# Hand order kept on the matrix engine alone, with a third matmul bank and earlier loads, in a fused windowed-attention and channel-mix kernel

**Chip, cores, metric.** One core of one Trainium2 chip. Times are microseconds (us) on the device. The kernel before took 222.08 us (median of 3 runs, 222.0 to 222.2).

Names: PE is the matrix engine, DVE VectorE, ACT ScalarE, POOL GpSimd, SP SyncE, and DMA a transfer. A *bank* is one of the eight banks of PSUM, the memory that takes PE's results. *Hand order* means that an engine runs its instructions in the order of the source; an engine that is not in hand order gets its order from the Tile scheduler when the program is built.

## The reference, cut

```python
# q, k, v: (4, 8, 768, 64) float32; n_sink 4, window 128
rel  = pos[:, None] - pos[None, :]
keep = (pos < 4) | ((rel >= 0) & (rel < 128))          # sink columns, and the window
a    = softmax(where(keep, q @ k.T / 8, -1e9))
x    = (a @ v), heads side by side                     # (4, 768, 512)
xk   = mu_k * x + (1 - mu_k) * x_prev                  # x_prev: the row before
xr   = mu_r * x + (1 - mu_r) * x_prev
out  = sigmoid(xr @ w_r) * (relu(xk @ w_k) ** 2 @ w_v) # w_k 512x1024, w_v 1024x512, w_r 512x512
```

## The kernel before: the parts that matter

Twelve units (4 batches times 3 blocks of 256 rows) of four attention steps each (c = 0 to 3, two heads a step). The channel mix of a unit is cut into ten chunks, which `fill` puts between the attention steps of the next units, so that PE always has work. The first four chunks, f0 to f3, are the products with w_k (tile mm); ACT makes rl of each and DVE kk. Two chunks give th, and four give the two halves of the output, o_sb. Cuts are marked `# ...`.

```python
tr_ps = ctx.enter_context(tc.tile_pool(name="tr_ps", bufs=2, space=PSUM))
o_ps = ctx.enter_context(tc.tile_pool(name="o_ps", bufs=2, space=PSUM))
mm_ps = ctx.enter_context(tc.tile_pool(name="mm_ps", bufs=2, space=PSUM))   # and sc_ps: 2 banks
# ...
load(0)
# ... constants on POOL, w_k's load on POOL's queue, mu_k and mu_r on ACT's
vs4 = const.tile([32, B, D + 1], FP32, name="vs4")            # v of the sink rows
for h in range(H):
    nc.sync.dma_start(out=vs4[4 * h:4 * h + 4, :, 0:D],
                      in_=v[:, h, 0:NS, :].rearrange("b s d -> s b d"))
# ... in prepare(u, part), for part == 2 of a batch's first unit:
            nc.gpsimd.tensor_tensor(out=vsink[b % 2][0:32, :, :], op=ALU.mult, in0=hmask,
                in1=vs4[:, b:b + 1, :].to_broadcast([32, H, D + 1]))
# ... def mix(u, half): four transposes of x, ACT's copy into xt, then
        td = x_pool.tile([128, 2, 256], BF16, name="td")
        nc.vector.tensor_tensor(out=td, in0=cur, in1=prv, op=ALU.subtract)
        for dst, mu in zip(mixed[u], (mu_k_sb, mu_r_sb)):     # xk twice, then xr twice
            for i in range(2):
                nc.vector.scalar_tensor_tensor(...)
# ...
    with tc.manual_schedule():                                # every engine in source order
        for part in range(4):
            prepare(0, part)
        load(1)
        # ... loads of w_r and w_v
        for n in range(N + LAG):
            u, c = divmod(n, NP)
            # ... sink_scores, scores(n)
            if 2 <= n < N + 2 and c % 2 == 1:
                mix((n - 2) // NP, ((n - 2) % NP) // 2)
            fill(n)
            if n < N:
                masked(n)                                     # DVE: e times the mask
            if 1 <= n < N + 1:
                values(n - 1)                                 # PE: o; DVE: rec, x
            fill(n)
            if n < N and u + 1 < U:
                prepare(u + 1, c)
                if c == 3 and u + 2 < U:
                    load(u + 2)
            if c % 2:
                fill(n)
            # ... n == 4: wv_h = 0.5 * wv_sb, eight DVE instructions
```

The softmax here doesn't subtract the row's maximum and nothing guards it: scores larger than these inputs give would overflow.

## Time and profile before

| what | value |
|---|---|
| time; span of the profiled run | 222.1; 220.4 us |
| PE busy | 180.1 us (82%) |
| first channel-mix matmul of unit 0 (its first f0) | 39.32 us |
| from there to the f0 of unit 11 | 168.23 us |
| from there to the end | 12.85 us |

The three last rows are first f0, stretch between the f0s, and tail. They are start times of the first matmul of w_k in a unit, read from PE's order of time. The lines of the profile stand in the prediction.

### The profile page before, as it was taken

How to read it: one execution, taken by the hardware profiler on the slowest of the kernel's cores; microseconds unless marked ns; L12 is line 12 of the kernel's file. 1: busy time of each engine (PE TensorE's matmuls, PEld its weight loads, DVE VectorE, ACT ScalarE, POOL GpSimd, SP SyncE). 2: the span in 40 equal slices, each digit the busy share in tenths (PEclk: the TensorE clock that was granted, in tenths of full speed). 3: DMA queues.
4: the chain of work that ended last, by engine and by line, in shares of the span. 5: the costliest groups of instructions: out<-in, count | busy, mean ns of one | idle time of the engine just before them, and what ended most of it. 6: DMA issues, size and time to landing. Idle time of an engine off the chain costs nothing.

```text
span 220.4 us, 4299 instructions
## 1 busy us (share of the span) xinstructions
PE 180.1 (82%) x1664; PEld 120.9 (55%) x1664; DVE 140.9 (64%) x344; ACT 124.9 (57%) x201; POOL 34.4 (16%) x69
## 2 busy tenths in 40 slices
PE   1705706999898898996997998988998989979892
PEld 1403405675765755854755757657557557555550
DVE  0011634976786678659669757857866696697632
ACT  2402703694675675774764956855757748555250
POOL 8736011223002001032020020050020200000000
PEclk9999985799999999999999999999999999999998
DMA  7979999950591991951782945915908911020202
GB/s 128 213 142 220 179 221 209 221 97 3 146 202 37 218 166 49 216 120 49 179 157 97 206 83 150 210 26 154 222 24 213 156 49 48 3 95 0 75 23 95
DMA packets 81668, 28.10 MB, mean 127 GB/s; under 512 B 76528, under 2 KB 78064, under 8 KB 81648
## 3 DMA queue, kind: packets, MB, share of 16 engines
q1 hardware_dynamic: 78496, 25.20, 52.6%
q0 software_dynamic: 2096, 2.62, 6.9%
q8 instruction: 13, 0.21, 0.4%
q10 hardware_dynamic: 1056, 0.00, 0.3%
q14 instruction: 7, 0.06, 0.1%
HBM read 24.15 MB, written 6.29 MB: 138 GB/s over the span
## 4 chain that ended last, share of the span: by engine, by line
PE 50%; DVE 16%; ACT 12%; DMA 11%; SPq 5%; issue 4%; ACTq 0%; DVEq 0%
PE mm L274 19%; PE mm L286 9%; DMA ks<-in_k_dram 6%; PE tps L151 6%; PE mm L294 6%; DVE xr L261 5%; SPq L69 4%; DMA vs<-in_v_dram 4%; ACT e L194 4%; DVE xk L261 4%; DVE o_sb L299 3%; PE sc L190 3%; ACT xt L253 3%; ACT rl L278 3%; DVE td L255 3%
## 5 line engine op out<-in xcount | busy, mean ns | idle before, releaser
L274 PE MATMUL mm<-xk,wk_sb 128*128 128x256 bf16 x384 | 50.1, 275 | 12.9 <-DVE o_sb L299 8.5
L194 ACT ACTIVATE e<-sc 128x1024 bf16<-128x1024 f32 (+1 forms) x48 | 46.0, 958 | 9.0 <-PE sc L190 9.0
L294 PE MATMUL mm<-wv_h,kk 128*128 128x512 bf16 x192 | 48.3, 379 | 0.0
L274 PEld LDWEIGHTS <-wk_sb 128*128 128x128 bf16 x384 | 36.4, 98 | 19.1 <-issue 14.6
L278 ACT ACTIVATE rl<-mm 128x512 bf16<-128x512 f32 x48 | 29.1, 607 | 29.2 <-PE mm L274 29.2
L156 POOL CAST v<-vs 128x512 bf16<-128x512 f32 x24 | 15.9, 664 | 139.5 <-DMA vs<-in_v_dram 83.7
L154 ACT CAST kt<-tps 128x512 bf16<-128x512 f32 x24 | 14.1, 586 | 41.5 <-PE tps L151 41.5
L255 DVE TENSOR_TENSOR td<-xt 128x512 bf16<-128x512 bf16 x24 | 10.6, 440 | 40.1 <-ACT xt L253 40.1
L151 PE MATMUL tps<-ident,ks 128*128 128x128 f32 x96 | 17.4, 312 | 20.1 <-DMA ks<-in_k_dram 20.1
L151 PEld LDWEIGHTS tps<-ident,ks 128*128 128x128 f32 x96 | 13.4, 161 | 24.3 <-issue 15.3
L286 PE MATMUL mm<-wr_sb,xr 128*128 128x512 bf16 x96 | 24.4, 380 | 0.0
L294 PEld LDWEIGHTS <-kk 128*128 128x128 bf16 x192 | 16.9, 98 | 13.1
L261 DVE SCALAR_TENSOR_TENSOR xk<-td,mu_k_sb,xt 128x256 bf16<-128x256 bf16 x48 | 23.2, 524 | 0.9
L279 DVE TENSOR_TENSOR kk<-rl 128x512 bf16<-128x512 bf16 x48 | 20.2, 421 | 5.4 <-ACT rl L278 3.9
L227 PE MATMUL o<-v,e 128*128 128x65 bf16 x352 | 21.0, 196 | 1.9 <-DVE e L203 1.3
L203 DVE TENSOR_TENSOR e<-e,mask 128x768 bf16<-128x768 bf16 x16 | 8.8, 551 | 21.5 <-ACT e L194 21.5
L200 DVE TENSOR_TENSOR e<-e,mask 128x1024 bf16<-128x1024 bf16 x32 | 22.3, 697 | 0.0
L261 DVE SCALAR_TENSOR_TENSOR xr<-td,mu_r_sb,xt 128x256 bf16<-128x256 bf16 x48 | 21.7, 492 | 0.0
L227 PEld LDWEIGHTS <-e 128*128 128x128 bf16 x352 | 17.7, 99 | 7.0 <-DVE e L200 1.9
L232 DVE TENSOR_TENSOR x<-o,rec 128x256 bf16<-128x256 f32 x48 | 20.4, 424 | 1.6
L190 PE MATMUL sc<-qt,kt 64*128 64x128 bf16 (+1 forms) x256 | 19.1, 251 | 0.7 <-ACT qt L154 0.7
L299 DVE SCALAR_TENSOR_TENSOR o_sb<-th,mm 128x512 f32<-128x512 f32 x24 | 16.2, 678 | 3.5 <-PE mm L294 3.5
(42 smaller groups left out, 166.6 us busy)
## 6 DMA issues: line engine op xcount, KB each, us to landing
ks<-in_k_dram SPq DMA_DIRECT2D x24, 256.0 KB
qs<-in_q_dram SPq DMA_DIRECT2D x24, 256.0 KB
vs<-in_v_dram SPq DMA_DIRECT2D x24, 256.0 KB
out_dram<-o_sb SPq DMA_DIRECT2D x24, 256.0 KB
wk_sb<-in_moe_w_k_dram POOLq DMA_DIRECT2D x1, 1024.0 KB, 9.7
wv_sb<-in_moe_w_v_dram POOLq DMA_DIRECT2D x1, 1024.0 KB, 13.9
wr_sb<-in_moe_w_r_dram POOLq DMA_DIRECT2D x1, 512.0 KB, 7.9
vs<-in_v_dram SPq DMA_DIRECT2D x8, 4.0 KB
```

Of the source, the lines that this page charges most:

```text
L151: nc.tensor.transpose(out=ps[:, c, :], in_=src[:, g, 2 * c:2 * c + 2, :].rearrange("p a d -> p (a d)"), identity=ident32)
L190: nc.tensor.matmul(out=sc[:, a, o0:o1], lhsT=lhs[rows], rhs=qt[rows, c, q0:q0 + o1 - o0], start=True, stop=True)
L194: nc.scalar.activation(out=e[:, :, lo:], in_=sc[:, :, lo:], func=AF.Exp, scale=scale)
L200: nc.vector.tensor_tensor(out=e, in0=e, in1=mask.rearrange("p a g k q -> p a (g k q)"), op=ALU.mult)
L227: nc.tensor.matmul(out=o[:, g, a, :], lhsT=e[:, a, e0:e0 + 128], rhs=rhs, start=(T == 0 and i == 0), stop=(i == len(blocks) - 1), skip_gro ...
L232: nc.vector.tensor_tensor(out=xs[u][:, :, 128 * c:128 * c + 128].rearrange("p g (a d) -> p g a d", a=2), in0=o[:, :, :, 0:D], in1=rec.to_b ...
L261: nc.vector.scalar_tensor_tensor(out=dst[:, c0 + i, :], in0=td[:, i, :], scalar=mu[:, c0 + i:c0 + i + 1], in1=prv[:, i, :], op0=ALU.mult, ...
L274: nc.tensor.matmul(out=ps[:, i, :], lhsT=wk_sb[:, c, 128 * f:128 * f + 128], rhs=xk[:, c, :], start=(c == 0), stop=(c == NC - 1), skip_gro ...
L278: nc.scalar.activation(out=rl, in_=ps, func=AF.Relu)
L286: nc.tensor.matmul(out=ps, lhsT=xr[:, c, 128 * g:128 * g + 128], rhs=wr_sb[:, c, :], start=(c == 0), stop=(c == NC - 1))
L294: nc.tensor.matmul(out=ps, lhsT=kk[:, f, 128 * g:128 * g + 128], rhs=wv_h[:, f, :], start=(f == 0), stop=(f == NF - 1))
L299: nc.vector.scalar_tensor_tensor(out=o_sb, in0=th[g], scalar=1.0, in1=ps, op0=ALU.add, op1=ALU.mult)
```

## The change

Its intent: leave only PE in hand order, let the Tile scheduler order the rest; bring load(1) forward; get the sink rows of v from tiles that are loaded anyway, by a matmul with a 0/1 matrix, instead of eight small loads and a POOL product; and give the channel mix a third bank, taken from o. In the source xk and xr are split, and xr is placed one step later.

```diff
-    o_ps = ... bufs=2        mm_ps = ... bufs=2
+    o_ps = ... bufs=1        mm_ps = ... bufs=3
     load(0)
+    load(1)
 ...
-    vs4 = ...; for h in range(H): nc.sync.dma_start(out=vs4[...], ...)
 ...
-            nc.gpsimd.tensor_tensor(out=vsink[b % 2][0:32, :, :], op=ALU.mult, in0=hmask, in1=vs4...)
+    def sink_values(b):
+        ps = tr_ps.tile([128, H, D], FP32, name="tps")
+        nc.tensor.matmul(out=ps, lhsT=spread, rhs=v_bufs[b * NT % 3][:, 0, :, 0:D], ...)
+        nc.vector.tensor_tensor(out=vsink[b % 2][0:32, :, 0:D], in0=ps[0:32], op=ALU.mult, in1=hmask...)
 ...
-    with tc.manual_schedule():
+    ORDERED = {mybir.EngineType.PE}
+    with tc.manual_schedule(engines=ORDERED):
 ...
-                mix((n - 2) // NP, ((n - 2) % NP) // 2)
+                transposed((n - 2) // NP, ((n - 2) % NP) // 2)
             fill; masked(n); values(n - 1)
+            if c % 2 == 1 and 2 <= n < N + 2:
+                mix((n - 2) // NP, ((n - 2) % NP) // 2, 0)          # td, xk
             fill
-                prepare(u + 1, c)
+                ... for u == 0 all four parts at c == 3, else prepare(u + 1, c)
+            if c % 2 == 0 and 3 <= n < N + 3:
+                mix((n - 3) // NP, ((n - 3) % NP) // 2, 1)          # xr, a step later
+            if c == 2 and inner and u % NT == 0:
+                sink_values(u // NT)
+            if n == 0: the loads of w_r and w_v
+            if n == 5: wv_h                                        # was n == 4
```

More of the change, by code (lines that the diff above doesn't have):

```diff
@@ L54 @@
     tr_ps = ctx.enter_context(tc.tile_pool(name="tr_ps", bufs=2, space=PSUM))
-    o_ps = ctx.enter_context(tc.tile_pool(name="o_ps", bufs=2, space=PSUM))
-    mm_ps = ctx.enter_context(tc.tile_pool(name="mm_ps", bufs=2, space=PSUM))
+    o_ps = ctx.enter_context(tc.tile_pool(name="o_ps", bufs=1, space=PSUM))
+    mm_ps = ctx.enter_context(tc.tile_pool(name="mm_ps", bufs=3, space=PSUM))
     raw = {}
@@ L107 @@
     nc.scalar.dma_start(out=mu_r_sb, in_=moe_mu_r.rearrange("(c p) -> p c", p=128))
-    vs4 = const.tile([32, B, D + 1], FP32, name="vs4")
-    for h in range(H):
-        nc.sync.dma_start(out=vs4[4 * h:4 * h + 4, :, 0:D],
-                          in_=v[:, h, 0:NS, :].rearrange("b s d -> s b d"))
     nc.gpsimd.memset(mask, 1.0)
@@ L129 @@
         nc.gpsimd.memset(t, 0.0)
-    hmask = const.tile([32, H, D + 1], FP32, name="hmask")
+    hmask = const.tile([32, H, D + 1], BF16, name="hmask")
     nc.gpsimd.memset(hmask, 1.0)
@@ L135 @@
                             pattern=[[4, H], [0, D + 1]], channel_multiplier=-1)
-    nc.gpsimd.memset(vs4[:, :, D:D + 1], 1.0)
+    for t in vsink:
+        nc.gpsimd.tensor_copy(out=t[0:32, :, D:D + 1], in_=hmask[:, :, D:D + 1])
+    spread = const.tile([128, 128], BF16, name="spread")
+    nc.gpsimd.memset(spread, 0.0)
+    nc.gpsimd.tensor_copy(out=spread[0:NS, 0:4 * H].rearrange("p (h s) -> p h s", s=NS),
+                          in_=ident[0:NS, 0:NS].unsqueeze(1).to_broadcast([NS, H, NS]))
     kts, qts = {}, {}
@@ L156, in prepare @@
             nc.gpsimd.tensor_copy(out=v_bufs[u % 3][:, g, :, 0:D], in_=vs[:, g, :, :])
-        if part == 2 and T == 0:
+        if part == 3 and T == 0:
             kz = ksink[b % 2].rearrange("p (c w) -> p c w", w=136)
@@ L162, in prepare @@
                                       in_=kts[u][rows, 0, :, 0:NS])
-            nc.gpsimd.tensor_tensor(
-                out=vsink[b % 2][0:32, :, :], op=ALU.mult, in0=hmask,
-                in1=vs4[:, b:b + 1, :].to_broadcast([32, H, D + 1]))
+    def sink_values(b):
+        ps = tr_ps.tile([128, H, D], FP32, name="tps")
+        nc.tensor.matmul(out=ps, lhsT=spread, rhs=v_bufs[b * NT % 3][:, 0, :, 0:D],
+                         start=True, stop=True)
+        nc.vector.tensor_tensor(out=vsink[b % 2][0:32, :, 0:D], in0=ps[0:32], op=ALU.mult,
+                                in1=hmask[:, :, 0:D])
     es, xs, live = {}, {}, {}
@@ L237, with transposed @@
     mixed = {}
-    def mix(u, half):
+    def transposed(u, half):
         b, T = divmod(u, NT)
@@ L250, in mix @@
         t0 = 2 + 256 * T
-        cur = xt[:, c0:c0 + 2, t0:t0 + 256]
+        nc.scalar.copy(out=xt[:, c0:c0 + 2, t0:t0 + 256], in_=ps)
+    def mix(u, half, which):
+        b, T = divmod(u, NT)
+        xt = xts[b % 2]
+        c0 = 2 * half
+        t0 = 2 + 256 * T
         prv = xt[:, c0:c0 + 2, t0 - 1:t0 + 255]
-        nc.scalar.copy(out=cur, in_=ps)
-        td = x_pool.tile([128, 2, 256], BF16, name="td")
-        nc.vector.tensor_tensor(out=td, in0=cur, in1=prv, op=ALU.subtract)
-        if half == 0:
+        if half == 0 and which == 0:
             mixed[u] = (x_pool.tile([128, NC, 256], BF16, name="xk"),
-                        x_pool.tile([128, NC, 256], BF16, name="xr"))
-        for dst, mu in zip(mixed[u], (mu_k_sb, mu_r_sb)):
-            for i in range(2):
-                nc.vector.scalar_tensor_tensor(
-                    out=dst[:, c0 + i, :], in0=td[:, i, :], scalar=mu[:, c0 + i:c0 + i + 1],
-                    in1=prv[:, i, :], op0=ALU.mult, op1=ALU.add)
+                        x_pool.tile([128, NC, 256], BF16, name="xr"),
+                        x_pool.tile([128, NC, 256], BF16, name="td"))
+        td = mixed[u][2][:, c0:c0 + 2, :]
+        if which == 0:
+            nc.vector.tensor_tensor(out=td, in0=xt[:, c0:c0 + 2, t0:t0 + 256], in1=prv,
+                                    op=ALU.subtract)
+        dst, mu = mixed[u][which], (mu_k_sb, mu_r_sb)[which]
+        for i in range(2):
+            nc.vector.scalar_tensor_tensor(
+                out=dst[:, c0 + i, :], in0=td[:, i, :], scalar=mu[:, c0 + i:c0 + i + 1],
+                in1=prv[:, i, :], op0=ALU.mult, op1=ALU.add)
     def ffn(u):
         b, T = divmod(u, NT)
-        xk, xr = mixed[u]
+        xk, xr, _ = mixed[u]
         kk = kk_pool.tile([128, NF, 256], BF16, name="kk")
@@ L310, with fill @@
     chunks = stream()
-    LAG = 6
     N = U * NP
-    def fill(n, count=1):
-        if n >= LAG:
-            for _ in range(count):
-                next(chunks, None)
-    with tc.manual_schedule():
+    def fill(count=1):
+        for _ in range(count):
+            next(chunks, None)
+    ORDERED = {mybir.EngineType.PE}
+    with tc.manual_schedule(engines=ORDERED):
         for part in range(4):
             prepare(0, part)
-        load(1)
-        nc.gpsimd.dma_start(out=wr_sb, in_=moe_w_r.rearrange("(c p) f -> p c f", p=128))
-        nc.gpsimd.dma_start(out=wv_sb, in_=moe_w_v.rearrange("(c p) f -> p c f", p=128))
-        for n in range(N + LAG):
+        for n in range(N + 6):
             u, c = divmod(n, NP)
-            if n < N:
+            inner = n < N
+            if inner:
                 if c == 0 and u % NT > 0:
@@ L330 @@
                 scores(n)
-            if 2 <= n < N + 2 and c % 2 == 1:
-                mix((n - 2) // NP, ((n - 2) % NP) // 2)
-            fill(n)
-            if n < N:
+            if c % 2 == 1 and 2 <= n < N + 2:
+                transposed((n - 2) // NP, ((n - 2) % NP) // 2)
+            if n >= 6:
+                fill()
+            if inner:
                 masked(n)
@@ L337 @@
                 values(n - 1)
-            fill(n)
-            if n < N and u + 1 < U:
-                prepare(u + 1, c)
+            if c % 2 == 1 and 2 <= n < N + 2:
+                mix((n - 2) // NP, ((n - 2) % NP) // 2, 0)
+            if n >= 6:
+                fill()
+            if inner and u + 1 < U:
+                if u == 0 and c == 3:
+                    for part in range(4):
+                        prepare(1, part)
+                elif u > 0:
+                    prepare(u + 1, c)
                 if c == 3 and u + 2 < U:
                     load(u + 2)
-            if c % 2:
-                fill(n)
-            if n == 4:
+            if c % 2 == 0 and 3 <= n < N + 3:
+                mix((n - 3) // NP, ((n - 3) % NP) // 2, 1)
+            if c == 2 and inner and u % NT == 0:
+                sink_values(u // NT)
+            if c % 2 and n >= 6:
+                fill()
+            if n == 0:
+                nc.gpsimd.dma_start(out=wr_sb, in_=moe_w_r.rearrange("(c p) f -> p c f", p=128))
+                nc.gpsimd.dma_start(out=wv_sb, in_=moe_w_v.rearrange("(c p) f -> p c f", p=128))
+            if n == 5:
                 for f in range(NF):
```

## The prediction

> **What bounds the kernel now.** I read the page first, for the shares and the granted clock; then the waits of the matrix engine in the steady stretch; then the order of time around one unit of work; then the start in slices of 1 us.
>
> The kernel runs 12 units (4 batches, 3 blocks of 256 rows), each with 4 attention steps (c = 0 to 3). The channel mix of a unit runs as 10 chunks between the attention steps of the next units: four chunks f0 to f3 (x times w_k, then rl and kk), two of th, and two of o in two halves each.
>
> ```profile
> PE 180.1 (82%) x1664; PEld 120.9 (55%) x1664; DVE 140.9 (64%) x344; ACT 124.9 (57%) x201; POOL 34.4 (16%) x69
> ...
> PE   1705706999898898996997998988998989979892
> ...
> PEclk9999985799999999999999999999999999999998
> DMA  7979999950591991951782945915908911020202
> ```
>
> PE is busy 82% of 220.4 us, and hardly less than 90% anywhere after slice 8 (44 us). So there are two losses: the start, up to about 40 us, and 10% of the rest. By the table of stretches PE is busy 147.7 of the 160 us between 40 and 200: 12.3 us idle. The waits say on what:
>
> ```profile
> PE mm L274 <- DVE o_sb L299: 7.6, 10, 1.4
> PE mm L274 <- ACT rl L278: 4.4, 10, 0.6
> PE o L227 <- DVE e L200: 0.2, 1, 0.2
> ```
>
> That is all of it: two waits per unit, each in front of a chunk f. The order of time in one unit (columns: start, us, engine, line, operation, tiles, idle before):
>
> ```profile
> 83.32 0.51 DVE L255 TENSOR_TENSOR td<-xt 128x512 bf16<-128x512 bf16 x1 [2.17 <-ACT xt L253]
> ...
> 84.67 0.88 DVE L261 SCALAR_TENSOR_TENSOR xr<-td,mu_r_sb,xt 128x256 bf16<-128x256 bf16 x2
> 85.46 0.68 DVE L299 SCALAR_TENSOR_TENSOR o_sb<-th,mm 128x512 f32<-128x512 f32 x1
> ...
> 86.19 1.03 PE L274 MATMUL mm<-xk,wk_sb 128*128 128x256 bf16 x8 [0.56 <-DVE o_sb L299]
> ...
> 87.97 1.03 PE L274 MATMUL mm<-xk,wk_sb 128*128 128x256 bf16 x8 [0.39 <-ACT rl L278]
> ```
>
> DVE does td, xk, xr, o_sb in that order, and f0 starts only when o_sb has emptied a bank. f1 then waits for rl of f0: the allocation of the built program gives f0 and f1 the same bank (in units 1 to 10). PE would have been ready for f0 at 86.19 - 0.56 = 85.63.
>
> The start is bound by loads:
>
> ```profile
> 14.00:15.00 1.00, 0.00 (x0) 0.00 (x0) 0.00 (x0) 0.00 (x0) 0.64 (x2) 1.00 0.38 65
> 15.00:16.00 1.00, 0.00 (x0) 0.00 (x0) 0.00 (x0) 0.00 (x0) 1.00 (x2) 1.00 0.02 4
> 16.00:17.00 1.00, 0.00 (x0) 0.00 (x0) 0.00 (x0) 0.00 (x0) 0.95 (x3) 1.00 0.25 58
> ...
> 33.15 2.12 DVE L348 TENSOR_SCALAR wv_h<-wv_sb 128x512 bf16<-128x512 bf16 x8 [3.38 <-DMA wv_sb<-in_moe_w_v_dram]
> ...
> 35.12 1.09 PE L151 MATMUL tps<-ident,ks 128*128 128x128 f32 x4 [6.63 <-DMA ks<-in_k_dram]
> ```
>
> The last columns of the slices are granted clock, DMA share and GB/s: 65, 4 and 58 GB/s, against some 190 to 275 around them, so about 2.4 us of DMA time are empty. There SP is busy issuing eight small loads of the sink rows (6.90 to 15.4 us), and the second unit's load stands behind them. PE waits 6.63 us for the third unit's ks at 35.12, then runs at half clock until 40.5.
>
> **What the Trainium skill says.** (1) "PSUM — Partial Sum Buffer", Specifications (TRN2): 8 banks per partition. The change spends the same eight: sc 2, tps 2, o 1 instead of 2, mm 3 instead of 2. (2) "SBUF — State Buffer", Who interferes with whom: a DVE instruction with two SBUF inputs contends with a GpSimd instruction that reads SBUF; it is a lock, held for the whole instruction. The trace agrees: beside the 1.43 us vsink product of POOL at 99.07 the pair of xk takes 1.70 us instead of 0.88, and f0 waits 1.35 us instead of 0.56. (3) "DMA: Bandwidth & Descriptors", Queues, rings and completion order: each DMA engine takes turns between the queues. It fits: with POOL's weight loads in flight (20 to 30 us) the sum stays at 189 GB/s, so weights and q, k, v hold each other up. (4) "TensorE: Matmul & The Clock Gate", Part 1: the clock is halved when idle and released by activity. The trace shows 0.50 from 31 to 40.5 us; the change does not remove this.
>
> **The change, part by part.**
>
> *Three mm banks.* In the program as built the banks rotate strictly: f0 takes the bank of th1, f1 that of the first o, f3 that of f0. The waits for o_sb and for rl of f0 before f1 go. What is then left before f0 is xk: its third and fourth matmuls wait for the two xk instructions of the later half.
>
> *The order of DVE.* The Tile scheduler now gives at c = 1: e, o_sb, rec, td, x, xk, xk, o_sb, xr, xr. xk is no longer ahead of e and o_sb, so I count it through with the trace's own spacing: exp ends at 82.81; e 0.61, o_sb 0.61, rec 0.21, td 0.46, x 0.35, xk twice 0.44 end at about 85.5 and 86.0. PE is ready at 85.63; its third and fourth matmuls come 0.21 and 0.32 later, 85.84 and 85.95. So f0 loses about 0.1 us instead of 0.56. Next, the transposes at c = 3 need x of the step before. DVE runs on without a gap: o_sb 0.61, xr 0.80, e 0.61, kk 0.38, rec 0.21, x 0.37 after 86.0 end at 89.0. PE, freed of both waits, would be there at 89.70 - 0.56 - 0.39 = 88.75. So some 0.2 to 0.3 us of the 0.95 come back as a wait for x. Per unit about 0.65 us are won, about 70%.
>
> Waits after 39 us are 8.5 + 4.4 + 0.6 = 13.5 us; 70% is **9.5 us**. The two units slowed by POOL's product (f0 at 102.62 and 149.36, 1.35 us each) are among them; with the product off POOL they become ordinary units.
>
> *Sink rows by matmul.* Four matmuls of 512 columns. Such a matmul costs 0.21 us (0.86 us for four of L286 in the chain), with its weights some 0.25; three lie in the steady stretch: **0.7 us** against us. Four DVE products of about 0.6 us each, beside PE. POOL loses 5.1 us, which is off the path but for the lock.
>
> *One o bank.* o of a step now waits for x of the step before. By the same counting x ends over 1 us before PE comes for the bank: no cost.
>
> *Early loads.* Without the eight small loads the 2.4 us hole fills, and the ks of unit 2 should land about 3 us earlier, near 32. But the scheduler puts four of the eight wv_h instructions ahead of rec and x of step 3 and e of step 4. They wait for wv_sb, which POOL issues only 1.1 us earlier (its vsink product is gone), so it lands near 32.0. Then: wv_h to 33.1, x to 34.0, e to 34.7, the transposes 34.6, xk complete about 38.2, against 39.66 before. Of 3 us, **about 1.6 us** remain.
>
> The tail after the last f0 (207.55 to 220.4) is the same work in the same order.
>
> Sum: 9.5 - 0.7 + 1.6 = 10.4 us off 222.1 gives 211.7; I say **211.5 us**.
>
> **Rivals.** (a) *The scheduler's order gives the gain back.* xk, now behind four other instructions, becomes the new wait before f0 as long as o_sb was. For it: DVE is 64% busy, and more once the units shorten; casts on POOL stretch xk by 0.2 us (1.11 for two at 68.40). Against: the count above leaves only 0.1 us. If f0 still waits 0.5 us and only the rl wait goes, the gain is 4.4 - 0.7 + 1.6: 216.8. (b) *The start gives all of it.* If wv_sb lands before it is needed, the ks arrival rules and 3 to 4 us are won, and with all 13.5 us of waits gone: 222.1 - 13.5 + 0.7 - 3.5 = 205.8. For it: PE is in hand order. Against: wv_h stands early in DVE's order. (c) *The loads are hidden anyway.* The start saves nothing since bytes bound it: 213.3. (d) *The single o bank stalls PE*, at 0.3 us per step, 48 steps: 14 us back, no gain. The slack above speaks against it.
>
> **Range and chances.** The middle of (a) and (b) is about where the sum lies. The range 207.0 to 216.5 leaves out the ends of both. Faster by over 2% means under 217.6, which even (a) reaches: 0.89. Same 0.09, for (d) in part; slower 0.02.
>
> **What would show it right or wrong.** Right: the waits of PE between 40 and 200 name o_sb and rl no more, or under 1 us each; 3 to 4 us remain, on xk and on x before the transposes; one unit takes 14.5 to 14.8 us from f0 to f0, against 15.2 to 16.4; no xk pair of 1.70 us beside POOL; no empty slices at 14 to 17 us; the wait of wv_h ends near 32 and the first f0 near 38. Wrong: waits of o on x (the single bank), a ks or v load late in the steady stretch since the queue's order changed, f0 waiting 0.5 us for xk in each unit, or a start that saves more than 3 us or nothing.

## The result

The changed kernel took 205.31 us (median of 4, 204.83 to 206.94) against 222.14 us of the kernel before on the same chip (4 runs, 222.0 to 222.81). Its outputs are correct. The ratio is 0.925, 95% interval 0.919 to 0.931. Ratios here and below are the mean time of one kernel's fast runs over the mean of the other's in the same rounds, so not quite the ratio of the medians quoted. A run counts as slow when it is over 1.5% above the fastest of its kernel; one kernel that also had slow runs is marked.

So it was faster, as predicted, but 205.3 lies below the range of 207.0 to 216.5: 6.2 us of gain more than I had said. The profiled span fell from 220.4 to 203.1 us:

| | before | after | difference |
|---|---|---|---|
| first f0 | 39.32 | 36.45 | -2.87 |
| to f0 of unit 11 | 168.23 | 153.80 | -14.43 |
| to the end | 12.85 | 12.85 | 0 |

The page of the changed kernel, the same four lines as of before:

```profile
PE 178.5 (88%) x1668; PEld 120.8 (59%) x1668; DVE 135.1 (66%) x348; ACT 125.3 (62%) x201; POOL 32.0 (16%) x68
...
PE   1717706899999999999999999999999999999992
...
PEclk9975755899999999999999999999999999999999
DMA  7999999998895995987879627402011020020202
```

PE worked 1.6 us less than before in a span 17.3 us shorter, so its share rose from 82 to 88%; its row reads 9 from slice 8 (counted from 0, as in the prediction) to the last but one. The DMA row has no 0 or 1 in the first slices. The granted clock still drops in slices 2 to 7; the prediction expected that to stay.

The waits of PE from 30 to 185 us (the columns are the time in total, how often, the longest):

```profile
PE tps L154 <- DMA ks<-in_k_dram: 7.3, 1, 7.3
PE tps L254 <- ACT qt L157: 0.7, 3, 0.2
PE mm L290 <- DVE xk L277: 0.4, 1, 0.4
PE tps L254 <- DVE x L239: 0.3, 1, 0.3
```

No wait for o_sb or rl is left. In the steady stretch 1.4 us remain in all, where the prediction expected 3 to 4. Half of that, the wait for qt, stands behind the three sink matmuls and is absent where these are taken out (a_vs4_between below).

One unit of the changed kernel in order of time, the stretch that answers to 83 to 88 us of the kernel before:

```profile
77.62 0.69 DVE L207 TENSOR_TENSOR e<-e,mask 128x1024 bf16<-128x1024 bf16 x1 [1.70 <-ACT e L201]
...
78.23 0.68 DVE L315 SCALAR_TENSOR_TENSOR o_sb<-th,mm 128x512 f32<-128x512 f32 x1
...
78.82 0.18 DVE L238 RECIPROCAL rec<-o 128x4 f32<-128x4 f32 x1
78.92 0.40 DVE L273 TENSOR_TENSOR td<-xt 128x512 bf16<-128x512 bf16 x1
...
79.23 0.42 DVE L239 TENSOR_TENSOR x<-o,rec 128x256 bf16<-128x256 f32 x1
...
79.56 0.87 DVE L277 SCALAR_TENSOR_TENSOR xk<-td,mu_k_sb,xt 128x256 bf16<-128x256 bf16 x2
...
80.01 0.39 PE L197 MATMUL sc<-qt,kt 64*128 64x256 bf16 x6
...
80.33 1.05 PE L290 MATMUL mm<-xk,wk_sb 128*128 128x256 bf16 x8
...
81.57 1.04 PE L290 MATMUL mm<-xk,wk_sb 128*128 128x256 bf16 x8
...
82.89 0.42 DVE L239 TENSOR_TENSOR x<-o,rec 128x256 bf16<-128x256 f32 x1
...
83.30 0.40 PE L254 MATMUL tps<-ident,x 128*128 128x128 bf16 x4
```

Read DVE's starts. e, o_sb, rec, td, x, xk: this is the order that the prediction took from the built program. But rec starts at 78.82 for 0.18 us, and td already at 78.92, before rec's record ends; x follows td by 0.31. In the kernel before, x stood next to rec and xk next to td, and started 0.21 and 0.55 us after them (86.66 to 86.87, 83.32 to 83.87). Here the independent td starts 0.10 us after rec, and x 0.31 after td, so less of DVE's time passes between the starts. f0 starts at 80.33, 0.32 us after the scores, without a wait. And x for the transposes at c = 3 is done at 82.89 + 0.42 = 83.31, while the transposes start at 83.30: they just meet.

The start, in slices of 1 us as before (last columns: granted clock, DMA share, GB/s), and two lines of the order of time:

```profile
14.00:15.00 1.00, 0.18 (x2) 0.16 (x2) 0.00 (x0) 0.00 (x0) 0.85 (x2) 0.50 1.39 219
15.00:16.00 1.00, 0.09 (x2) 0.00 (x0) 0.00 (x0) 0.00 (x0) 1.00 (x3) 0.50 1.38 217
16.00:17.00 1.00, 0.81 (x8) 0.35 (x7) 0.50 (x2) 0.10 (x1) 0.94 (x5) 0.50 1.39 217
```

```profile
30.27 0.90 DVE L376 TENSOR_SCALAR wv_h<-wv_sb 128x512 bf16<-128x512 bf16 x4 [7.98 <-DMA wv_sb<-in_moe_w_v_dram]
...
32.25 1.09 PE L154 MATMUL tps<-ident,ks 128*128 128x128 f32 x4 [7.29 <-DMA ks<-in_k_dram]
```

The hole at 14 to 17 us is filled: 217 to 219 GB/s instead of 65, 4 and 58. The wait for the third unit's ks ends at 32.25 instead of 35.12, 2.87 us earlier, exactly what the first f0 gained. wv_sb arrived for wv_h at 30.27, not 32.0.

### The profile page after: what moved, and what is told of

Same layout as the page of the kernel before. It is cut to its first block, busy times and chain, and to the rows that moved or that the text cites. A ratio compares the mean times of both kernels' runs of the same rounds, so it can differ in the third digit from the quotient of the medians.

```text
span 203.1 us, 4308 instructions
## 1 busy us (share of the span) xinstructions
PE 178.5 (88%) x1668; PEld 120.8 (59%) x1668; DVE 135.1 (66%) x348; ACT 125.3 (62%) x201; POOL 32.0 (16%) x68
## 4 chain that ended last, share of the span: by engine, by line
PE 67%; DVE 11%; SPq 9%; DMA 7%; ACT 4%; issue 2%; DVEq 0%
PE mm L290 17%; PE mm L310 15%; PE mm L302 11%; SPq L69 9%; PE tps L154 7%; DMA ks<-in_k_dram 7%; PE sc L197 5%; PE o L234 4%; PE tps L254 3%; DVE o_sb L315 3%; DVE xk L277 2%; PE o L223 2%; PE tps L181 2%; ACT e L201 2%; DVE xr L277 2%
## 5 line engine op out<-in xcount | busy, mean ns | idle before, releaser
L201 ACT ACTIVATE e<-sc 128x1024 bf16<-128x1024 f32 (+1 forms) x48 | 45.9, 957 | 14.5 <-PE sc L197 12.7
L290 PEld LDWEIGHTS <-wk_sb 128*128 128x128 bf16 x384 | 34.7, 98 | 6.2 <-issue 1.8
L159 POOL CAST v<-vs 128x512 bf16<-128x512 f32 x24 | 18.1, 767 | 112.6 <-PE o L234 53.7
L234 PEld LDWEIGHTS <-e 128*128 128x128 bf16 x352 | 18.2, 100 | 8.7 <-issue 3.9
L154 PEld LDWEIGHTS tps<-ident,ks 128*128 128x128 f32 x96 | 13.5, 161 | 16.1 <-issue 7.4
L277 DVE SCALAR_TENSOR_TENSOR xk<-td,mu_k_sb,xt 128x256 bf16<-128x256 bf16 x48 | 21.2, 477 | 0.0
L197 PEld LDWEIGHTS <-kt 64*128 64x128 bf16 x256 | 8.9, 95 | 15.2 <-issue 14.6
## 6 DMA issues: line engine op xcount, KB each, us to landing
wv_sb<-in_moe_w_v_dram POOLq DMA_DIRECT2D x1, 1024.0 KB, 12.9
```

The costliest lines, as they stand in the source:

```text
L154: nc.tensor.transpose(out=ps[:, c, :], in_=src[:, g, 2 * c:2 * c + 2, :].rearrange("p a d -> p (a d)"), identity=ident32)
L197: nc.tensor.matmul(out=sc[:, a, o0:o1], lhsT=lhs[rows], rhs=qt[rows, c, q0:q0 + o1 - o0], start=True, stop=True)
L201: nc.scalar.activation(out=e[:, :, lo:], in_=sc[:, :, lo:], func=AF.Exp, scale=scale)
L234: nc.tensor.matmul(out=o[:, g, a, :], lhsT=e[:, a, e0:e0 + 128], rhs=rhs, start=(T == 0 and i == 0), stop=(i == len(blocks) - 1), skip_gro ...
L277: nc.vector.scalar_tensor_tensor(out=dst[:, c0 + i, :], in0=td[:, i, :], scalar=mu[:, c0 + i:c0 + i + 1], in1=prv[:, i, :], op0=ALU.mult, ...
L290: nc.tensor.matmul(out=ps[:, i, :], lhsT=wk_sb[:, c, 128 * f:128 * f + 128], rhs=xk[:, c, :], start=(c == 0), stop=(c == NC - 1), skip_gro ...
```

## The experiments

The first question is what ended the waits for o_sb and rl: the third bank, or the order of DVE? The kernel before with the bank split alone:

```diff
# the kernel before, but
-    o_ps bufs=2, mm_ps bufs=2
+    o_ps bufs=1, mm_ps bufs=3
```

> The kernel before with the bank split of the changed kernel alone (o 1 bank, mm 3), DVE and ACT still in hand order. Theory A, the order theory: the third bank takes away the two waits before f0 and f1, but in the hand order (td, xk, xr, o_sb, e, rec, x, o_sb, kk, e, rec, x without a gap) x of step c = 1 still ends only 0.1 to 0.3 us sooner, and the transposes at c = 3 wait for it; 0.3 us per unit, so 217 to 220 us, with a new wait of the transposes on x of 5 us or more in all. Theory B, the bank theory of the prediction: the waits go and hardly anything comes in their place, 12 to 14 us off, so 208 to 211 us.

Measured: 222.11 us (221.38 to 222.85), ratio 1.001 [0.997, 1.005]. Nothing at all. The waits of PE from 40 to 185 us:

```profile
PE o L216 <- DVE x L232: 10.1, 11, 1.5
PE o L227 <- DVE x L232: 1.8, 3, 0.6
```

The two old waits are gone, and o now waits for x instead, 11.9 us in all: the single o bank is not free, because in the hand order x still comes late. This is my rival (d), which I had dismissed; it is true, but only with the old order of DVE. A third mm bank beside two of o was not run, since the eight banks are spent. The trace of the kernel before leaves little to win by it: DVE works from td at 83.32 to the end of x at 89.53 with no gap over 0.07 us, and the transposes that need this x start at 89.70. Next the reverse, the changed kernel with two mm banks and two of o:

```diff
# the changed kernel, but
-    o_ps bufs=1, mm_ps bufs=3
+    o_ps bufs=2, mm_ps bufs=2
```

> The changed kernel with the banks of before (o 2, mm 2). Theory A (order): o_sb of both halves ends before f0 and f1 come to their banks, so at most 1 us is lost: 205 to 207 us. Theory B (banks): the wait of f0 for o_sb and one more per unit come back, 10 us or more: 214 to 218 us.

Measured: 205.43 us (205.19 to 206.44), ratio 0.9255 [0.923, 0.929], the same as the changed kernel. PE waits from 40 to 185 us for nothing of the channel mix:

```profile
PE tps L254 <- ACT qt L157: 0.7, 3, 0.2
PE tps L254 <- DVE x L239: 0.3, 1, 0.3
```

So this split of the banks is worth nothing with either order. The scheduler alone, on the unchanged source:

```diff
# the kernel before, but
-    with tc.manual_schedule():
+    with tc.manual_schedule(engines={mybir.EngineType.PE}):
```

> The kernel before with hand order on PE alone and nothing else changed (mm 2 banks, sink loads and the product on POOL as before). The built program now rotates the two mm banks strictly (f0 and f1 no longer share one), and DVE does e, td, o_sb, xk, xk, xr, xr, rec, o_sb, x. Theory A (order): o_sb empties the bank before f0 comes, rl of f0 is no longer waited for; nearly all of the 14 us of the steady stretch is won, less some for the product on POOL: 208 to 212 us. Theory B (banks): with two banks the waits of f0 on o_sb and of f1 stay, 219 to 223 us.

Measured: 208.28 us (207.6 to 208.52), ratio 0.937 [0.935, 0.940]. This one line makes some 14 of the 17 us. The first f0 comes at 37.81, the next stretch takes 154.63 us. Which engine's order is it? Only DVE left to the scheduler:

```diff
# the kernel before, but
-    with tc.manual_schedule():
+    with tc.manual_schedule(engines={PE, Activation, Pool, SP})      # of mybir.EngineType
```

> The kernel before in hand order on every engine but DVE, whose order alone the scheduler sets; two mm banks, the old sink rows and loads. Theory A (the gain of the steady stretch is DVE's order, with the bank rotation that follows from it): the waits of PE for o_sb and rl fall from 13 us to under 3, 208 to 212 us. Theory C (it takes ACT, POOL or SP in scheduled order too): 215 us or more.

Measured: 211.69 us (211.07 to 213.33), ratio 0.953 [0.947, 0.959]; first f0 at 38.82, the stretch 157.40 us, so DVE's order alone takes 10.8 us out of it. From 40 to 185 us PE waits for the mm banks still, but little:

```profile
PE mm L274 <- DVE o_sb L299: 3.4, 8, 0.8
```

And the counterpart, all but PE and DVE left to the scheduler:

```diff
# the kernel before, but
+    with tc.manual_schedule(engines={PE, DVE})                       # of mybir.EngineType
```

> The kernel before with hand order on PE and VectorE, and ScalarE, GpSimd and SyncE by the scheduler. The built program still gives f0 and f1 one bank. Order theory: the steady stretch stays as before (12 to 14 us of waits for o_sb and rl after 39 us), only the start may move by 1 us: 220 to 222.5. Rival (the scheduler's order on ScalarE or GpSimd has its own part in the gain): under 218, waits under 9 us.

Measured: 221.26 us (220.31 to 221.85), ratio 0.994 [0.991, 0.998]. The waits from 40 to 185 us are smaller for o_sb than before (6.9 us there, in the same window), but the stretch between the f0s is 167.99 us, hardly shorter:

```profile
PE mm L274 <- DVE o_sb L299: 4.5, 9, 0.7
PE mm L274 <- ACT rl L278: 4.0, 9, 0.6
```

Two waits that are not shown, for x and for e, add 1.1 and 0.9 us. So the gain needs the other order of DVE, and the others' order is worth about 1 us without it and some 3.4 us on top of it (211.69 to 208.28, each against the kernel before).

One rival was left. With DVE scheduled, the built program also deals the two mm banks strictly in turn; with DVE in hand order, f0 and f1 share one (this can be read from the allocation of each built program; the traces fit: in b_dve f1 starts up to 0.44 us before rl of f0 ends, while before it waits for rl in each of units 1 to 10). So DVE's order might work only by way of the banks. The kernel before with strictly alternating banks and everything in hand order:

```diff
# the kernel before, but
-    mm_ps: one pool of 2
+    mm_pools: two pools of 1, taken in turn, tile by tile
```

> The kernel before, in hand order on all engines, with its two mm banks taken strictly in turn (two pools of one buffer). f0 then takes the bank of the first o half, f1 that of the second o half, so f1 no longer waits for rl of f0. If the shared bank was the cause (bank theory), both waits go: 209 to 217 us, rl not named any more, o_sb under 2 us in all. If VectorE's hand order is the cause (order theory): o_sb of the second half ends at 87.89 in the trace of before whatever PE does, since VectorE runs without a gap from td at 83.32 to there, and f1 started at 87.97. So f1 waits for o_sb until about the same time: 219 to 223 us, and the wait only changes its name from rl to o_sb.

Measured: 222.47 us (221.42 to 223.41), ratio 1.000 [0.996, 1.005]. The waits from 40 to 185 us, and the three lines of one unit:

```profile
PE mm L283 <- DVE o_sb L308: 11.0, 18, 1.5
```

```profile
85.71 1.03 PE L283 MATMUL mm<-xk,wk_sb 128*128 128x256 bf16 x8 [0.78 <-DVE o_sb L308]
...
86.73 0.68 DVE L308 SCALAR_TENSOR_TENSOR o_sb<-th,mm 128x512 f32<-128x512 f32 x1
...
87.46 1.03 PE L283 MATMUL mm<-xk,wk_sb 128*128 128x256 bf16 x8 [0.36 <-DVE o_sb L308]
```

The wait for rl is gone, and a wait for the second o_sb stands in its place, of the same size: the total is 11.0 us, as 6.9 + 4.0 were before. DVE runs its td, xk, xr, o_sb, e, rec, x, o_sb without a gap, and whichever bank f1 gets, the one instruction that empties it ends at the same time. So with the old order the dealing of the banks is worth nothing: the order of DVE was the cause, and the shared bank only gave the wait its name. Not tested is the new order of DVE with f0 and f1 in one bank. In the changed kernel rl of f0 ends at 82.02 us, 0.44 after f1 has started (0.44 to 0.62 in units 1 to 10), so a shared bank would have held f1 back by some 5 us in all (an estimate from these ends). The alternation that came with the scheduler's order may thus be a condition of the gain, though alone it brings none.

Is it the scheduler that is needed, or an order? The changed kernel in hand order on all engines:

```diff
# the changed kernel, but
-    with tc.manual_schedule(engines=ORDERED):
+    with tc.manual_schedule():
```

> The changed kernel with hand order on all engines (the source's own order: o_sb, e, rec, x, td, xk, xk, o_sb, kk, e, rec, x). Theory A (order): DVE's dependent pairs (rec and x, td and xk) stand next to each other and each pays its latency, and o_sb at the head of the list waits for PE; 0.2 to 0.5 us per unit come back before f0 and before the transposes: 207 to 211 us. Theory B (banks): the third bank does it, the order is of no account: 204 to 206 us.

Measured: 211.35 us (208.84 to 213.11), ratio of the fast runs 0.942 [0.938, 0.946]. Two of its four runs were slow (212.9 and 213.1), the profiled one among them, so I do not read small differences from its profile; the two fast ones took 208.8 and 209.8. So the new source gets about 13 of the 17 us in its own hand order. It places xr a step later, but it also loads earlier and has no POOL product; these parts were not run one by one in hand order. Even in the slow run the stretch takes 159.41 instead of 168.23 us, so most of the gain is not the start. A better order counts, whoever makes it; the scheduler's is some 4 us better still.

The second question is the start. First, was wv_h the brake, as the prediction had it? The changed kernel without wv_h (0.5 goes into rl's scale as a square root, since rl is squared):

```diff
# the changed kernel, but
-    wv_h = 0.5 * wv_sb; o from wv_h; rl = Relu(mm)
+    o from wv_sb; rl = Relu(sqrt(0.5) * mm)
```

> The changed kernel without the eight wv_h instructions on DVE: the factor 0.5 goes into the scale of rl (the root of 0.5, then squared), o reads wv_sb. It takes away what I held to be the brake of the start in the prediction, the wait of DVE for wv_sb. If wv_h was the brake, the first f0 comes 1 us or more earlier, 203 to 204 us. If the third unit's ks is the brake, as the trace of the changed kernel says (PE waits 7.29 us for it, wv_h ends before), nothing changes: 204.5 to 206 us.

Measured: 205.0 us (204.84 to 205.97), ratio 0.9225 [0.917, 0.928]. No difference that can be told from the changed kernel's 205.31, and its first f0 comes at 37.56, not earlier than 36.45: wv_h was no brake. Next, the sink rows as before, but in the new kernel:

```diff
# the changed kernel, but
     load(0)
+    vs4's eight small loads
     load(1)
-    sink_values(b): matmul and DVE product
+    the POOL product of vs4 and hmask, in prepare
```

> The changed kernel with the old sink rows: eight small loads of v between the first and the second unit's load, and the product with the mask on POOL. Theory D (the start gains by the hole in the DMA queue): the hole at 14 to 17 us is back, the first f0 comes 1 to 2.5 us later, and in the steady stretch one or two xk pairs are stretched beside POOL's product: 207 to 209 us. Theory E (the start gains by something else, such as the weights issued earlier): 205 to 206 us.

Measured: 206.4 us (205.88 to 206.85), ratio 0.928 [0.923, 0.933]; only 1.1 us is lost by the medians, 1.5 by the profiled spans. The hole at 14 to 17 us is back (56, 6 and 82 GB/s). But two effects almost cancel: the first f0 comes at 39.0, 2.55 us later than in the changed kernel, and the stretch after it takes 152.70 us, 1.10 less. So in these two profiled runs the early loads are worth 2.5 us (a_fold's 37.56, with the same loads, shows that single runs differ by 1 us here), and the three steady sink matmuls, with what goes with them, cost 1.1. A sink matmul in the changed kernel (L169) takes 0.38 us alone, not the 0.21 that I had taken from matmuls standing in a row, and the wait for qt behind it adds 0.23. The units with one take 14.66, 14.42 and 14.41 us in the changed kernel, and 13.91, 14.00 and 13.90 here; two other units take 0.23 more here.

What then does the start wait for? My theory after these runs: bytes. Ahead of the third unit's ks stand 3 MB of q, k and v and 1 MB of w_k, and ks itself has 0.5 MB; but the weights w_r and w_v (1.5 MB) share the engines with them. At about 0.2 MB per us 1.5 MB are 7.5 us (an estimate from the 217 GB/s above). So let them wait:

```diff
# a_fold, but
-    ORDERED = {PE}
+    ORDERED = {PE, Pool}
-            if n == 0: loads of w_r and w_v
+            if n == 3: loads of w_r and w_v     # in POOL's order behind the casts of unit 1's v
```

> As a_fold, and POOL in hand order with the loads of w_r and w_v issued behind the casts of the second unit's v, so behind its landing. If the start is bound by the bytes in front of the third unit's ks, and the weights are among them, ks of unit 2 lands near 24 us instead of 32, the first f0 comes near 29 instead of 36.5, and the time is 197 to 200 us, with PE perhaps waiting once for wr_sb or wv_sb. If the start is bound by something else, 204 to 206 us.

Measured: **197.51 us** (197.29 to 199.07, 5 runs), ratio 0.888 [0.883, 0.894]. It beats both kernels. The clock row of its page, and PE's first work on the third unit's ks and the first f0:

```profile
PEclk9999999999999999999999999999999999999999
```

```profile
25.47 0.63 PE L153 MATMUL tps<-ident,ks 128*128 128x128 f32 x4
...
28.39 0.39 PE L289 MATMUL mm<-xk,wk_sb 128*128 128x256 bf16 x2
```

ks is there when PE comes, at 25.47, without a wait (32.25 in the changed kernel), and the clock is never halved for long enough to show in the row. Its load was issued no earlier (19.15 us, against 18.64 in the changed kernel), but landed 5.0 us after that instead of 13.5, so it is the bytes beside it that counted. POOL's hand order came with the edit and was not run alone. The first f0 moves from 36.45 to 28.39, 8.1 us: 6.8 because PE starts on ks earlier, and 1.3 because from there to f0 it takes 2.92 us at a granted clock of 1.00 instead of 4.20 at 0.50. Some 2.3 come back in the stretch (156.10 us, most of it in the first unit, where PE waits 1.07 us for xk inside f0 and 0.98 for the fourth unit's ks). One step further, w_k too behind the casts of unit 0's v:

```diff
# a_weights_last, but
-    load of w_k among the constants
+    load of w_k behind prepare(0, ...) in POOL's order
```

> a_weights_last with the load of w_k as well issued behind the casts of unit 0's v on GpSimd. If the start is bound by the bytes ahead of what is needed next, v of unit 0 comes about 3 us earlier (PE waited for its cast to 15.98), and so does all behind it: first f0 at 25 to 26 instead of 28.4, 194.5 to 196 us. Rival: w_k (1 MB, 10.7 us from issue to landing) is then itself what the first f0 waits for, and nothing or little is won: 196.5 to 199 us.

Measured: 198.69 us (197.78 to 199.17), ratio 0.892 [0.889, 0.896], so nothing is won. The clock row of its page, and three lines of its order of time, in the columns of before:

```profile
PEclk9999859999999999999999999999999999999999
```

```profile
12.37 0.51 PE L232 MATMUL o<-v,e 128*128 128x65 bf16 x6 [0.17 <-POOL ksink L162]
...
24.13 1.09 PE L152 MATMUL tps<-ident,ks 128*128 128x128 f32 x4 [2.22 <-DMA ks<-in_k_dram]
...
28.33 0.61 PE L288 MATMUL mm<-xk,wk_sb 128*128 128x256 bf16 x2
```

The first half of the theory held: o of unit 0 starts at 12.37 instead of 15.98, since v is there. But the third unit's ks lands at 24.00, no earlier than in a_weights_last (24.17), since w_k's bytes only changed their place ahead of it. PE, now early, waits 2.22 us for it, and from 22.8 to 29.6 us the granted clock is 0.50. So from ks to f0 it takes 4.20 us again (24.13 to 28.33) instead of 2.92, and the first f0 is at 28.33, the same as 28.39. PE starts on ks 1.34 us earlier and loses 1.28 of that to the clock. For the landing of ks only those bytes are worth moving that can stand behind it.

## Why the prediction was wrong in size

The direction, the filled hole and the end of the two waits were right; the sum was short by 6.2 us. The term that was mis-sized most is the 9.5 us for the waits: measured, it is 14.43 us off the stretch and the 1.1 that the sink matmuls cost in it, 15.5 in all. Step by step:

- **"Per unit about 0.65 us are won, about 70%" failed.** I took 30% of the waits off for "some 0.2 to 0.3 us of the 0.95" coming back before the transposes at c = 3. I had counted DVE's chain with the old spacing of dependent instructions, 6.10 us from e to the end of the second x. It took 5.69 (77.62 to 83.31), because the new order puts independent work between rec and x and between td and xk. Of the 13.5 us, 0.7 remained (waits for xk and x; the 0.7 for qt belongs to the sink matmuls below) instead of 4.0: **3.3 us** of the miss.
- **The size of the waits themselves was under-read.** A wait starts where PE's last record ends, and that end is modelled. Of the kernel before:

```profile
85.24 0.40 PE L190 MATMUL sc<-qt,kt 64*128 64x256 bf16 x6
```

f0 follows at 86.19, 0.95 us after these scores start. Without a stall it follows by 0.32 (80.01 to 80.33 in the changed kernel), so the stall was 0.63 and not the 0.56 of the record. In front of f1 the same difference, from the last o matmuls on, is 0.56 against 0.39 (87.06 to 87.97 before, 81.22 to 81.57 after). So a unit lost 1.19 us, not 0.95; for ten units that is **2.4 us** more to win (the same comparison in each of units 1 to 10 adds up to this too).
- **"So it lands near 32.0 ... about 1.6 us remain" failed.** POOL issued the load of wv_sb at 17.32 instead of 19.22, 1.9 us earlier and not 1.1, and it took 12.9 instead of 13.9 us, so wv_h began at 30.27; and taking it out changes nothing (a_fold). The start gave 2.87 instead of 1.6: **1.3 us**.
- **"Four matmuls of 512 columns. Such a matmul costs 0.21 us" was too low.** 0.7 us predicted, 1.1 by a_vs4_between: -0.4 us.

Together 3.3 + 2.4 + 1.3 - 0.4 = 6.6 us. By the profiled spans there are 6.9 to explain (17.3 gained, 10.4 in the sum); 6.2 is the distance of the median from the rounded 211.5. The split is worked out from single profiled runs, so a few tenths in each are open, and more in the start: the first f0 lies at 36.45, 36.73 and 37.56 in three kernels with the new loads (the changed one, a_two_banks, a_fold), and at 38.67 to 39.32 in three with the old (b_rotate, b_banks, the kernel before). Also open is how much of the stretch came from the clock: before, it was regained at 41.2 us (the prediction read 40.5), 1.9 us after the first f0; in the changed kernel at 36.6, 0.1 us after it.

- **The reason named for the largest part was wrong, although the waits went as it said.** "*Three mm banks* ... the waits for o_sb and for rl of f0 before f1 go": b_banks and b_rotate show that with the old order of DVE neither this split of the banks nor their dealing was worth anything, and a_two_banks that with the new order the split is not. I had treated the order of DVE as a possible cost of the change; it was its gain.
- **"One o bank ... no cost"** held in the changed kernel and failed in b_banks (11.9 us of waits): it holds only with the new order.
- **Right:** the hole filled, ks near 32, o_sb and rl named no more, no slow xk pair (0.87 us in each unit that was slow before, against 1.70), the tail unchanged. Of the other signs, a unit from f0 to f0 takes 13.61 to 14.66 us (units 1 to 9), where 14.5 to 14.8 stood, and the first f0 comes at 36.45 and the end of wv_h's wait at 30.27, where 38 and 32 stood. "Hardly less than 90% anywhere after slice 8" was read loosely: the row has a 6 and 7s there. Rival (b), 205.8 us, is what came about, through other causes in part.

## What to carry to other kernels

When PE waits for a bank, look first at when the engine that empties it gets to that instruction, and in which order it works: if it is busy without a gap, as DVE was here, another bank only renames the wait. A wait read from the profile was too small here, because the record before it ends by a model; compare start to start with the same stretch where nothing waits. At the start, sort loads by the moment of their first use, and keep back those, and only those, which can stand behind it. Look at the granted clock beside each wait: the same work from ks to the first f0 took 2.92 us at 1.00 and 4.20 at 0.50.

## What the Trainium skill lacked or had wrong

- "Perfetto Trace Analysis", Matmuls, advises that independent matmul groups rotate through different banks. It lacks that rotation is worth nothing while the emptying engine is late: 222.11 us with the third bank taken from o and 222.47 with strict rotation, against 222.1 without. What a shared bank costs once that engine is early was not run.
- The same page, Tensor Engine Instruction, says that the end of a matmul is estimated. It lacks the consequence, which fits the trace: idle times read from such ends were short by 0.07 us in front of f0 and 0.17 in front of f1.
- "VectorE: DVE Perf Modes", The DRAIN you can't avoid, says that the next instruction does not start until the pipe is empty, and that one which is not held starts earlier. This trace shows the latter: td starts at 78.92, before the end of rec's record at 79.00, and x, which needs rec, 0.41 us after rec's start while td fits in between. It lacks the advice to put an independent instruction between two dependent ones.
- "DMA: Bandwidth & Descriptors", Queues, rings and completion order: the taking of turns between queues fits the runs (ks takes 13.5 us from issue to landing beside the 1.5 MB of weights, and 5.0 with these held back). It lacks the advice that follows, to delay the issue itself.
